# Attention followed by a mixture of experts, one core: other buffers and another order at the hand-over, and one more weight split on GpSimd

## The chip, the cores and the metric

The kernel runs on one core of one Trainium2 chip. The metric is the device time of one execution in microseconds, as the median of several runs; the profile is of one further execution of the same program. The engines are named as in the profile: PE is TensorE (PEld its weight loads), DVE is VectorE, ACT is ScalarE, POOL is GpSimd, and SP issues most of the DMAs.

## What is computed

Eight batches of eight heads, 576 positions, head dimension 64: rotary embedding, softmax attention, and then, on the 4608 rows of 512 columns that come out, a mixture of eight experts in which each row goes to the one expert with the largest gate logit. Input scales (`q`, `k`, and the output gate) are raised by constant factors, so that rounding in a single pass would change which expert is chosen.

```python
q_rot, k_rot = (rotate(q), rotate(k))
scores = scale * np.matmul(q_rot, k_rot.transpose(0, 1, 3, 2))
scores = scores - np.max(scores, axis=-1, keepdims=True)
attn = np.exp(scores)
attn = attn / (np.sum(attn, axis=-1, keepdims=True) + 1e-09)
out = np.matmul(attn, v)                      # (8, 8, 576, 64) -> x (4608, 512)
...
logits = x @ w_gate
e_idx = np.argmax(logits, axis=1)
gate_w = probs[np.arange(N), e_idx]           # softmax of logits
eom = 1.0 / (1.0 + np.exp(-(x @ w_output_gate)))
for e in range(E):
    mask = e_idx == e
    h = np.maximum(x[mask] @ w1[e], 0.0)
    ye = h @ w2[e]
    out[mask] = gate_w[mask, None] * eom[mask, e, None] * ye
```

## The kernel before

**Attention half.** The work is cut into 32 pairs of heads (8 batches, 4 pairs each), numbered from 0, and each pair into 9 row units. A unit's scores `sc` (L502) are sums of products of high and low parts (`kh`, `kl` against `q`, which holds both parts of the queries); DVE takes the row maximum `m` (L507), ACT the exponential `pm` (L516), DVE a blockwise transpose `pt` (L522), and PE the product with the values into `acc`: 288 small matmuls a pair (L544, forms of 160 and 128 columns). Behind a pair ACT evicts `acc` to `ac`, PE turns it back to rows with the matrix `ii` (the step `back`, L559), and DVE divides it into `xb` (`divide`, L571), the rows of the layer's input `x` together with the gate numbers.

Ahead of a pair, SP loads its raw queries and keys as two DMAs of 0.59 MB each into one tile `raw` of two buffers (`load`, L433: t = 1 the key half, t = 0 the query half). GpSimd multiplies and adds the rotary factors in place (L445 and behind it), and ACT and GpSimd write the high and low parts (L419, L427): `kl` is the last reader of the key half, `q` the last reader of the query half. SP also loads `v` (`loadv`, L440, four DMAs a pair).

What is issued when is a table: `EVENTS` gives for each step of a pair an offset in row units from the pair's start, and `att.step(g)` issues everything that stands at unit g. `att.G` is the unit behind the last pair's last maximum; `att.rest(...)` issues what is left over after it. The steps that the change names stand there as

```python
("load1", -18, 1), ("load0", -15, 1), ... ("loadv0", 5, 2), ("loadv1", 7, 2),
("evict", 17, 2), ("newxb", 18, 1), ("back", 19, 1), ("divide", 19, 2),
```

`place` finds for the rows of a batch the places in the expert lists and issues the stores of `xb` to `xd` in DRAM (L667, L669), three a batch, from which GpSimd gathers the experts' rows later. Of the last batch the list steps stand in `att.last`: first the one-hot rows `ro` (ACT, L719 and L720, five pairs of instructions), then the products with them, and `lists` (L746) at the end.

**MoE half.** The lists are worked off in 26 slots, a double one of 256 rows or a single one of 128. The first 5 doubles are made from the lists of the first six batches and so may begin before the last batch is through; behind them come 9 doubles mixed with 12 singles. A slot gathers its rows `xg` by GpSimd (L1039), PE transposes them (`turn`, `mtp` L1069), ACT and DVE copy them as high and low `xt` (L1084, L1085), four first products `ph` follow (`first`, L1096 and L1104), a relu on ACT, and four second products `py` (`second`, L1146), which GpSimd scatters to `out` (L1158). In a single slot the relu rows are transposed by PE in between (`across`, tile `htp`, L1131) and copied by ACT and DVE as `ht` (L1132, L1133). Each of a slot's eight weights `wr` is loaded by SP (L1052), eight loads ahead, and split six ahead into `wh` (ACT, L1061) and `wl` (L1063); `wl` is DVE's work, and in single slots GpSimd takes two of the eight (j = 1 and 5).

**PSUM.** The scores have a pool of two tiles of their own, `ps_s`; `acc` stands in `ps_a`. A small ring `Small` gives its tiles to `mtp`, `htp` and the list steps alike. When the scores are through, `ps_s` is closed, and the small ring and `ph` move to its place.

**The hand-over.** It is written out by hand: `moe.begin0` (the expert numbers `0ei`, four weights, the gathers of slots 0 and 1), the first transposes `turned_in(0, 0)`, the leftovers of attention up to unit G+1 with `back` of pair 30, `turned_in(0, 1)`, `turn`, three splits, the product of pair 31, `first(0, 0)`, `back` of pair 31 and the list product, then `first(0, 1)` and the slots.

## Time and profile before

| what | value |
|---|---|
| median of 3 runs | 1017.67 us (1014.06 to 1022.49) |
| profiled execution | 1021.62 us, of which the span is 1019.8 |
| mean granted clock of PE | 0.992 |
| busy: PE, PEld, DVE, ACT, POOL | 94%, 83%, 79%, 64%, 59% of the span |
| HBM | 198.64 MB read, 22.43 MB written, 217 GB/s |
| the hand-over | about 490 to 530 us in the span |

The span is the time from the first to the last instruction in the trace; the rest of an execution's time, 1.8 us here, lies around it. PE's 94% is an average over two halves and holds matmuls that wait for a part of their operands; it doesn't say in which places PE is late. Clock figures such as 0.82 are shares of PE's full speed.

### The profile page before, as it was taken

How to read it: one execution, taken by the hardware profiler on the slowest of the kernel's cores; microseconds unless marked ns; L12 is line 12 of the kernel's file. 1: busy time of each engine (PE TensorE's matmuls, PEld its weight loads, DVE VectorE, ACT ScalarE, POOL GpSimd, SP SyncE). 2: the span in 40 equal slices, each digit the busy share in tenths (PEclk: the TensorE clock that was granted, in tenths of full speed). 3: DMA queues.
4: the chain of work that ended last, by engine and by line, in shares of the span. 5: the costliest groups of instructions: out<-in, count | busy, mean ns of one | idle time of the engine just before them, and what ended most of it. 6: DMA issues, size and time to landing. Idle time of an engine off the chain costs nothing.

```text
span 1019.8 us, 34668 instructions
## 1 busy us (share of the span) xinstructions
PE 960.9 (94%) x14461; PEld 842.6 (83%) x14461; DVE 801.0 (79%) x1186; ACT 657.2 (64%) x1370; POOL 604.2 (59%) x626
## 2 busy tenths in 40 slices
PE   4989999989999999898889999999999999999995
PEld 4778878878878788787788898898998989898894
DVE  6779988989989899898759777667777776867772
ACT  4656677777867768676465455457567765856762
POOL 4768998998999989989521113135315343533621
PEclk9989999999999999999999999999999999999998
DMA  6546566566746757654559767768787887988860
GB/s 223 159 124 189 170 186 175 164 194 173 219 129 206 214 150 202 186 178 120 182 198 340 280 201 240 217 193 300 289 305 234 330 291 251 343 277 267 301 238 30
DMA packets 58208, 221.00 MB, mean 217 GB/s; under 512 B 9351, under 2 KB 9660, under 8 KB 53952
## 3 DMA queue, kind: packets, MB, share of 16 engines
q1 hardware_dynamic: 50304, 196.37, 61.2%
q0 software_dynamic: 6464, 21.26, 5.5%
q8 instruction: 115, 1.88, 0.8%
q10 hardware_dynamic: 1280, 1.11, 0.3%
q14 instruction: 45, 0.37, 0.1%
HBM read 198.64 MB, written 22.43 MB: 217 GB/s over the span
## 4 chain that ended last, share of the span: by engine, by line
PE 42%; DVE 3%; issue 3%; DMA 2%; ACT 1%; POOL 1%; POOLq 0%; ACTq 0%; DVEq 0%
PE py L1146 18%; PE ph L1104 15%; PE ph L1096 5%; DVE wl L1063 2%; PE mtp L1069 2%; DMA wr<-in_w 1%; PE acc L544 1%; PE htp L1131 1%; DMA out<-y,2idx 1%; PE sc L502 1%; ACT wh L1061 1%; DVE ht L1133 0%; PE acc L559 0%; DVE ht L1121 0%; DVE xt L1085 0%
## 5 line engine op out<-in xcount | busy, mean ns | idle before, releaser
L516 ACT ACTIVATE pm<-sc,m 128x576 f32<-128x576 f32 x288 | 211.8, 739 | 138.0 <-DVE m L507 119.3
L1063 DVE TENSOR_TENSOR wl<-wr,wh 128x1024 fp32r<-128x1024 f32 x184 | 253.9, 1392 | 44.5 <-ACT wh L1061 42.5
L507 DVE TENSOR_REDUCE m<-sc 128x1 f32<-128x576 f32 x288 | 206.7, 753 | 50.0 <-PE sc L502 48.2
L502 PE MATMUL sc<-kh,q 64*128 64x288 f32 x1024 | 202.5, 327 | 22.4 <-ACT q L419 9.4
L1146 PE MATMUL py<-wh,ht 128*128 128x512 f32 x640 | 214.4, 400 | 0.0
L544 PE MATMUL acc<-pt,v 32*64 32x160 f32 (+1 forms) x9216 | 201.0, 298 | 14.0 <-issue 9.0
L1061 ACT CAST wh<-wr 128x1024 fp32r<-128x1024 f32 x208 | 212.6, 1050 | 0.9 <-DMA wr<-in_w 0.9
L522 DVE STREAM_TRANSPOSE pt<-pm 128x576 f32<-128x576 f32 x288 | 207.2, 753 | 0.0
L502 PEld LDWEIGHTS sc<-kh,q 64*128 64x128 f32 x1024 | 151.1, 192 | 52.6 <-ACT pm L516 19.1
L544 PEld LDWEIGHTS acc<-pt,v 32*64 32x64 f32 x9216 | 160.0, 132 | 39.3 <-issue 30.4
L445 POOL TENSOR_TENSOR raw<-raw,rt 128x1152 f32<-128x1152 f32 x62 | 164.1, 2647 | 0.2
L1104 PE MATMUL ph<-xt,wh 128*128 128x256 f32 x896 | 160.8, 282 | 0.5 <-DVE xt L1085 0.5
L1104 PEld LDWEIGHTS ph<-xt,wh 128*128 128x128 f32 x896 | 138.2, 188 | 2.6 <-DVE xt L1085 1.4
L1146 PEld LDWEIGHTS py<-wh,ht 128*128 128x128 f32 x640 | 120.3, 188 | 24.1
L502 PE MATMUL sc<-kl,q 64*128 64x288 f32 x512 | 128.8, 305 | 0.5 <-issue 0.5
L1104 PE MATMUL ph<-xt,wl 128*128 128x256 f32 x448 | 125.8, 281 | 0.0
L1146 PE MATMUL py<-wl,ht 128*128 128x512 f32 x320 | 125.0, 391 | 0.0
L1063 POOL TENSOR_TENSOR wl<-wr,wh 128x1024 fp32r<-128x1024 f32 x24 | 58.7, 2444 | 86.7 <-ACT wh L1061 83.0
L1120 ACT ACTIVATE ht<-ph 128x512 fp32r<-128x512 f32 x56 | 33.5, 598 | 86.3 <-PE ph L1104 86.3
L449 POOL TENSOR_TENSOR raw<-raw 128x576 f32<-128x576 f32 x62 | 87.8, 1416 | 1.8
L502 PEld LDWEIGHTS sc<-kl,q 64*128 64x128 f32 x512 | 87.4, 193 | 0.2 <-DVE kl L427 0.2
L1104 PEld LDWEIGHTS ph<-xt,wl 128*128 128x128 f32 x448 | 84.4, 188 | 0.1
(249 smaller groups left out, 1323.7 us busy)
## 6 DMA issues: line engine op xcount, KB each, us to landing
wr<-in_w SPq DMA_DIRECT2D x208, 512.0 KB
raw<-in_qk SPq DMA_DIRECT2D x64, 576.0 KB
v<-in_v SPq DMA_DIRECT2D x128, 288.0 KB
xd<-xb SPq DMA_DIRECT2D x16, 640.0 KB
xd<-xb SPq DMA_DIRECT2D x8, 160.0 KB
rt<-in_rope ACTq DMA_DIRECT2D x1, 576.0 KB
xg<-xd,2idx POOLq DMA_INDIRECT x18
out<-y,2idx POOLq DMA_INDIRECT x18
```

The lines of the kernel that those rows point to most:

```text
L445: self.eng(eng).tensor_tensor(out=rv, in0=rv, in1=self.rt[:, 2 * t:2 * t + 2, x], op=ALU.mult)
L449: self.eng(eng).tensor_tensor(out=r[:, 2 * t, x], in0=r[:, 2 * t, x], in1=r[:, 2 * t + 1, x], op=ALU.add)
L502: self.nc.tensor.matmul(self.ps[i][:, a, :HS], st, mov[r, x], start=(n == 0), stop=(n == 2))
L507: nc.vector.tensor_reduce(self.m[i], ps[:, :, :HS], axis=AX.XY, op=ALU.max, negate=True)
L516: nc.scalar.activation(pe.rearrange("p (a b) -> p a b", a=2), self.ps[i][:, :, :HS], AF.Exp, bias=self.m[i], scale=1.0, accum_out=self.z[: ...
L522: self.nc.vector.transpose(out=self.pt[:, st[0] + 5 * st[1] if st else 4, :], in_=self.pc.pop(i))
L544: nc.tensor.matmul(self.acc[h * D:h * D + D, a, o:o + 32 * n], self.v[r, h, j, :], self.pt[r, u:u + n, 32 * j:32 * j + 32], start=(j == 0) ...
L1061: self.nc.scalar.copy(wh, r)
L1063: eng.tensor_tensor(out=wl, in0=r, in1=wh.bitcast(F32), op=ALU.subtract)
L1096: nc.tensor.matmul(ph[:, 0, :], st[:, dc, 0:P], mv[:, dc, :], start=(n == 0), stop=(n == 11))
L1104: nc.tensor.matmul(ph[:, f, :], st[:, dc, fs], mv[:, dc, :], start=(n == 0), stop=(n == 11))
L1146: self.nc.tensor.matmul(py[h], st[:, f, hs], mv, start=(f == 0 and n == 0), stop=(f == 7 and n == 2))
```

## The change

There are seven edits.

1. The tile `raw` is replaced by two, `raw1` (keys) and `raw0` (queries), of two buffers each, from a new pool `pr2` that stays open to the end. Each half is a tile that its load waits for by itself.
2. The first four weights of every eight (`u % 8 < 4`) are loaded into these `raw` buffers. The first four of all are issued from the attention's table, at the places where a pair 32 and a pair 33 would load their halves; `begin0` no longer stands at the hand-over.
3. The `acc` of the last pair gets a pool of its own, `ps_e`, in the scores' banks; the small ring and `ph` move to the place of `ps_a`, which is closed behind `back` of pair 30. With it the order of the hand-over changes: leftovers up to unit G+4 stand ahead of the transposes of slot 0.
4. The gathers of slot 1 stand behind `lists` and behind a copy of one element, `past`, that reads the last pair's `ac`.
5. The `xd` stores of batches 6 and 7 are issued in the slots (pieces 30, 34, ... of the list of leftovers), and no longer ahead of them.
6. The tile `htp` has two banks of its own in the pool `pm`, and no longer comes from the small ring.
7. In a single slot GpSimd also makes the `wl` that is split at j = 3. (The split is six ahead: this is the second weight of the next slot, so that it is an addition where that is a double one, which happens seven times.)

```diff
@@ the pools
-    early, main, scores = ExitStack(), ExitStack(), ExitStack()
+    early, main, scores, sums, ends = (ExitStack() for _ in range(5))
...
+    pr2 = pool(ctx, "pr2", 2, side="right")
     pp1, pp2 = pool(early, "pp", 1, side="right"), pool(early, "pp2", 2, side="right")
-    ps_a = pool(main, "ps_a", 1, space=PSUM, side="left")
+    ps_a = pool(sums, "ps_a", 1, space=PSUM, side="left")
@@ the hand-over
         att.at(g + 6, 2, moe.fetch)
+        for u, k in enumerate(("load1", "load0", "load1", "load0")):
+            att.at(att.G + 9 * (u // 2) + dict((n, o) for n, o, _ in EVENTS)[k], 1, lambda u=u: moe.load(u))
+    moe.raws = pr2
...
-        moe.begin0()
     for g in range(att.G, att.G + TURN):
         att.step(g)
     scores.close()
-    small.move(pool(ctx, "ps_x", 2, space=PSUM, side="right", reuse_waits="tile"))
-    moe.ph = pool(ctx, "ps_h", 1, space=PSUM, side="right", reuse_waits="tile")
+    att.pairs[-1].ps_a = pool(ends, "ps_e", 1, space=PSUM, side="right", reuse_waits="tile")
+    att.rest(lambda g: g <= att.G + 1)
+    sums.close()
+    small.move(pool(ctx, "ps_x", 2, space=PSUM, side="left", reuse_waits="tile"))
+    moe.ph = pool(ctx, "ps_h", 1, space=PSUM, side="left", reuse_waits="tile")
...
+        att.rest(lambda g: g <= att.G + 4)
         moe.turned_in(0, 0)
-        att.rest(lambda g: g <= att.G + 1)
         moe.turned_in(0, 1)
...
         att.rest(lambda g: True)
+        nc.gpsimd.tensor_copy(moe.t([1, 1], "past"), att.pairs[-1].ac[0:1, 0, 0, 0:1])
+        moe.gather(1)
         main.close()
         moe.first(0, 1)
+    ends.close()
     moe.open_left(pool(ctx, "ml", 1, side="left", reuse_waits="tile"),
-                  pool(ctx, "ps_m", 1, space=PSUM, side="left", reuse_waits="tile"))
+                  pool(ctx, "ps_m", 1, space=PSUM, side="right", reuse_waits="tile"))
     if n0:
         left = att.last + pieces(moe.table1(), 72)
+        for k, f in enumerate(att.later):
+            k = 30 + 4 * k
+            left[k] = lambda f=f, g=left[k]: (g(), f())
@@ the raw halves
+    @staticmethod
+    def rawtile(pr2, t, name):
+        return pr2.tile([P, 2, S], F32, tag=f"raw{t}", name=name)
...
     def load(self, t):
-        if t:
-            self.raw = self.pp2.tile([P, 4, S], F32, tag="raw", name=f"raw{self.nm}")
-        self.nc.sync.dma_start(out=self.raw[:, 2 * t:2 * t + 2, :], in_=self.qkd[:, 2 * t:2 * t + 2, :])
+        self.raw[t] = self.rawtile(self.pr2, t, f"raw{self.nm}_{t}")
+        self.nc.sync.dma_start(out=self.raw[t], in_=self.qkd[:, 2 * t:2 * t + 2, :])
@@ the stores of the last two batches
-    stores = lambda: [store(i) for i in range(3)]
     if last:
+        later += [lambda i=i: store(i) for i in range(3)]
...
-        fs += [(37, 2, lambda: (s13(), stores()))]
+        fs += [(37, 2, s13)]
+        later += [lambda i=i: store(i) for i in range(3)]
@@ the weights
         self.gather(0)
-        self.gather(1)
...
-        self.wr[u] = self.buf("wr", u, self.LOADS, 4, [P, 1024], F32, f"wr{u}{self.nm}")
+        if u % self.LOADS < 4:
+            t = Pair.rawtile(self.raws, 1 - u % 2, f"wr{u}{self.nm}")
+            self.wr[u] = t.rearrange("p a b -> p (a b)")[:, 0:1024]
+        else:
+            self.wr[u] = self.buf("wr", u, self.LOADS, 4, [P, 1024], F32, f"wr{u}{self.nm}")
...
-    def split(self, u):
+    def split(self, u, help=False):
...
-        eng = self.nc.gpsimd if self.todo[s][0] == 1 and j % 4 == 1 else self.nc.vector
+        eng = self.nc.gpsimd if help or self.todo[s][0] == 1 and j % 4 == 1 else self.nc.vector
@@ the relu rows of a single slot
-        tp = self.small.tile(f"htp{s}_{j}{self.nm}")
+        tp = self.pm.tile([P, 4, P], F32, tag=f"htp{j % 2}", name=f"htp{s}_{j}{self.nm}")
@@ the slot
-            self.split(u + self.LEAD)
+            self.split(u + self.LEAD, single and j == 3)
```

How this moves instructions is shown at three places. A row reads: line, operation, what it writes and reads, and its shape. The numbers behind names tell tiles of the same name apart.

**SP in the first pairs, with the engines that each row waits for.** The `v` tiles are those of pairs 1 and 2, the `raw` rows the two halves of pair 4, which use a buffer of pair 2. Before:

```order
L440 DMA v_462<-in_v 32x2304 [waits DMAHW2_49]
L440 DMA v_462<-in_v 32x2304 [waits DMAHW3_49]
L433 DMA raw_607<-in_qk 128x1152 [waits DMAHW4_49,Pool_49]
L433 DMA raw_607<-in_qk 128x1152 [waits DMAHW5_49]
L440 DMA v_754<-in_v 32x2304 [waits DMAHW6_49,PE_49]
```

After, the same place:

```order
L456 DMA v_469<-in_v 32x2304 [waits DMAHW2_49]
L456 DMA v_469<-in_v 32x2304 [waits DMAHW3_49]
L449 DMA raw_1_614<-in_qk 128x1152 [waits DMAHW4_49,Pool_49]
L449 DMA raw_0_687<-in_qk 128x1152 [waits DMAHW5_49,Pool_49]
L456 DMA v_762<-in_v 32x2304 [waits DMAHW6_49,PE_49]
```

Before, the key half's row waits for `Pool` for the tile as a whole, and the query half follows it; now each row has a wait for `Pool` of its own.

**PE and SP at the hand-over.** First PE, before: `acc_9652` is pair 30 and `acc_9961` pair 31, `mtp_0` and `mtp_1` are the transposes of slot 0.

```order
L544 MATMUL acc_9652<-pt_9209,v_9455 64x128
L544 MATMUL acc_9652<-pt_9209,v_9455 64x160
L1069 MATMUL mtp_0_9917<-ident,xg 128x128 x4
L559 MATMUL acc_9652<-ii,ac_113 128x160 x5
L1069 MATMUL mtp_1_9935<-ident,xg 128x128 x4
L544 MATMUL acc_9961<-pt_9590,v_9760 64x160
L544 MATMUL acc_9961<-pt_9590,v_9760 64x128
```

After, at the same place (`acc_9696` and `acc_9964` are the two pairs now):

```order
L560 MATMUL acc_9696<-pt_9244,v_9503 64x128
L560 MATMUL acc_9696<-pt_9244,v_9503 64x160
L575 MATMUL acc_9696<-ii,ac_117 128x160 x5
L560 MATMUL acc_9964<-pt_9632,v_9806 64x160
L560 MATMUL acc_9964<-pt_9632,v_9806 64x128
```

And behind the 128th matmul of pair 31, some 45 rows later:

```order
L560 MATMUL acc_9964<-pt_9632,v_9806 64x128
L560 MATMUL acc_9964<-pt_9632,v_9806 64x160
L1089 MATMUL mtp_0_10035<-ident,xg 128x128 x4
L1089 MATMUL mtp_1_10040<-ident,xg 128x128 x4
L560 MATMUL acc_9964<-pt_9632,v_9806 64x160
```

The product of pair 31 follows `back` of pair 30 directly, and both transposes stand inside it, behind 128 of its 288 matmuls. Now SP, before; the `v` tile is pair 31's:

```order
L440 DMA v_9760<-in_v 32x2304 [waits DMAHW4_49,DMAHW5_49,DMAHW2_49,PE_49]
L440 DMA v_9760<-in_v 32x2304 [waits DMAHW3_49]
L440 DMA v_9760<-in_v 32x2304 x2
L1050 TENSOR_LOAD 0ei [waits Pool_49]
L1050 ISA x2
L1052 ISA
L1052 DMA wr_9901<-in_w 128x1024 [waits DMAHW6_49]
L1052 ISA
L1052 DMA wr_9903<-in_w 128x1024 [waits DMAHW7_49]
```

After, around the `v` tiles of pairs 30 and 31:

```order
L1072 DMA wr_9277<-in_w 128x1024 [waits DMAHW6_49,Pool_49]
L1072 ISA
L1072 DMA wr_9416<-in_w 128x1024 [waits DMAHW7_49,Pool_49]
L456 DMA v_9503<-in_v 32x2304 [waits DMAHW0_49,PE_49]
L456 DMA v_9503<-in_v 32x2304 [waits DMAHW1_49]
L456 DMA v_9503<-in_v 32x2304 [waits DMAHW2_49]
L456 DMA v_9503<-in_v 32x2304 [waits DMAHW3_49]
L1072 ISA
L1072 DMA wr_9655<-in_w 128x1024 [waits DMAHW4_49,Pool_49]
L1072 ISA
L1072 DMA wr_9729<-in_w 128x1024 [waits DMAHW5_49,Pool_49]
L456 DMA v_9806<-in_v 32x2304 [waits DMAHW6_49,PE_49]
```

The four weights `wr` went ahead of the `v` rows of pair 30 and pair 31, in twos, each with a wait for GpSimd.

**POOL at a single slot that a double one follows.** `xg` is a gather, `out` a scatter. Before:

```order
L1063 TENSOR_TENSOR wl_12225<-wr_12176,wh_12224 128x1024
L1039 DMA xg<-xd,2idx 128x640 x2
L1063 TENSOR_TENSOR wl_12296<-wr_12269,wh_12295 128x1024
L1158 DMA out<-y_12301,1idx 4608x512
L1039 DMA xg<-xd,1idx 128x640
L1158 DMA out<-y_12491,1idx 4608x512
L1063 TENSOR_TENSOR wl_12634<-wr_12571,wh_12633 128x1024
```

After:

```order
L1083 TENSOR_TENSOR wl_12266<-wr_12217,wh_12265 128x1024
L1055 DMA xg<-xd,2idx 128x640 x2
L1083 TENSOR_TENSOR wl_12337<-wr_12310,wh_12336 128x1024
L1178 DMA out<-y_12342,1idx 4608x512
L1083 TENSOR_TENSOR wl_12452<-wr_12403,wh_12451 128x1024
L1055 DMA xg<-xd,1idx 128x640
L1178 DMA out<-y_12532,1idx 4608x512
L1083 TENSOR_TENSOR wl_12675<-wr_12612,wh_12674 128x1024
```

One `wl` was added, between the scatter of a single slot and a gather.

## Rows read from the trace of the kernel before

**Rows 1.** PE's waits, whole span: engine, releaser: us in total, times, longest us.

```profile
PE acc L544 <- issue: 9.0, 11, 3.6
...
PE mtp L1069 <- DVE ht L1133: 2.8, 4, 0.8
```

**Rows 2.** Maxima of pairs 2, 3 and 31: stretch, us, DVE busy, PEclk, DMA share, GB/s.

```profile
45.81:64.67 18.86, 6.44 (x9) 0.82 0.63 184
66.72:79.40 12.68, 6.44 (x9) 1.00 0.54 147
492.45:509.92 17.47, 6.45 (x9) 0.90 0.70 237
```

**Rows 3.** PE timeline in pair 2: start, us, instructions, [idle before <- releaser].

```profile
59.08 2.39 PE L544 MATMUL acc<-pt,v 32*64 32x160 f32 x50 [3.56 <-issue]
```

**Rows 4.** DMA queues from 44.4 to 56.4 us: packets, MB, share of 16 engines.

```profile
q1 hardware_dynamic: 478, 2.36, 76.8%
```

**Rows 5.** POOL timeline of the first pairs: last readers of the two raw halves.

```profile
37.04 1.41 POOL L427 TENSOR_TENSOR kl<-raw,kh 128x576 fp32r<-128x576 f32 x1 [2.41 <-ACT kh L419]
...
42.75 1.41 POOL L427 TENSOR_TENSOR q<-raw,q 128x576 fp32r<-128x576 f32 x1 [4.29 <-ACT q L419]
```

**Rows 6.** SP timeline, 473 to 516 us: the issues at the hand-over.

```profile
473.49 18.00 SPq L440 DMA_DIRECT2D v<-in_v  x8
492.56 2.00 SPq L1052 DMA_DIRECT2D wr<-in_w  x4
515.45 0.90 SPq L667 DMA_DIRECT2D xd<-xb  x2
```

**Rows 7.** PE timeline at the hand-over.

```profile
511.98 1.63 PE L559 MATMUL acc<-ii,ac 128*128 128x160 f32 x10 [0.36 <-ACT ac L553]
...
514.74 3.74 PE L544 MATMUL acc<-pt,v 32*64 32x160 f32 x196 [0.70 <-DVE xb L571]
520.21 1.88 PE L544 MATMUL acc<-pt,v 32*64 32x160 f32 x92 [1.72 <-issue]
...
524.95 1.52 PE L559 MATMUL acc<-ii,ac 128*128 128x160 f32 x10
...
527.26 0.51 PE L1104 MATMUL ph<-xt,wh 128*128 128x256 f32 x2
...
538.86 0.60 PE L1069 MATMUL mtp<-ident,xg 128*128 128x128 f32 x4
```

**Rows 8.** ACT timeline: at the hand-over, and in a lone single slot.

```profile
514.56 2.94 ACT L1061 CAST wh<-wr 128x1024 fp32r<-128x1024 f32 x3
517.40 0.53 ACT L719 ACTIVATE ro<-row,hr 128x288 fp32r<-128x288 bf16 x1
...
747.36 1.06 ACT L1061 CAST wh<-wr 128x1024 fp32r<-128x1024 f32 x1
```

**Rows 9.** POOL timeline: pair 31's `q`, `lists`, and one weight split.

```profile
490.18 1.40 POOL L427 TENSOR_TENSOR q<-raw,q 128x576 fp32r<-128x576 f32 x1
...
528.88 0.80 POOL L746 TENSOR_TENSOR lists<-lc,lists 128x288 f32<-128x288 f32 x1 [13.46 <-ACT lc L743]
...
699.38 2.44 POOL L1063 TENSOR_TENSOR wl<-wr,wh 128x1024 fp32r<-128x1024 f32 x1
```

**Rows 10.** DVE timeline around two single slots that a double one follows.

```profile
700.47 2.43 DVE L1063 TENSOR_TENSOR wl<-wr,wh 128x1024 fp32r<-128x1024 f32 x1 [0.53 <-ACT wh L1061]
...
716.79 0.68 DVE L1085 TENSOR_TENSOR xt<-mtp,xt 128x512 fp32r<-128x512 f32 x1
...
749.94 1.23 DVE L1063 TENSOR_TENSOR wl<-wr,wh 128x1024 fp32r<-128x1024 f32 x1
...
752.89 0.69 DVE L1085 TENSOR_TENSOR xt<-mtp,xt 128x512 fp32r<-128x512 f32 x1
```

**Rows 11.** PE timeline: the first two matmuls of the two double slots.

```profile
717.60 0.40 PE L1104 MATMUL ph<-xt,wh 128*128 128x256 f32 x2
...
753.46 0.55 PE L1104 MATMUL ph<-xt,wh 128*128 128x256 f32 x2
```

More of the change, by code (lines that the diff above doesn't have):

```diff
@@ L273, in __init__ @@
         self.todo = {}
[L274 removed]
+        self.last, self.later = [], []
         at = self.at
@@ L578, in number, with place @@
     return float(b * S - m + (b * S >= m))
-def place(tc, pools, pairs, b, NT, cc, trib, oneb, cnt, xbs, xd, row, lists):
+def place(tc, pools, pairs, b, NT, cc, trib, oneb, cnt, xbs, xd, row, lists, later):
     nc = tc.nc
```

37 lines of the change are left out of this document (18 added, 19 removed).

## The prediction

> **What bounds the kernel now.** I read the list of TensorE's waits first, then stretches that hold the same work at several places, then the order of time there. TensorE waits for very little that another engine owes it: in the MoE half the largest entry is 2.8 us, four waits of the token transposes `mtp` for DVE; in the attention half, past the wait for the first query, the largest is 9.0 us in eleven waits marked "issue", where TensorE waited for nothing that the profile shows [rows 1]. So what counts is not a share of busy time but single places where TensorE is late.
>
> The second view takes the nine row maxima of one head pair: 12.68 us in an ordinary pair, 18.86 us in pair 2 and 17.47 us in pair 31, the last one [rows 2]. The maxima themselves cost the same 6.44 us each time; the other engines were waiting. In pair 2 TensorE stands still for 3.56 us with "issue" [rows 3]. In the 12 us before, the DMA engines moved 2.36 MB of `raw` and `v` in 478 packets on q1, and no packet of the instruction queue q8 [rows 4]. I read this as TensorE out of instructions, its next block queued behind data that was issued earlier. The same reading fits pair 31, where `v` is issued up to 491.5 and the four weights from 492.56 [rows 6], and the wait of 1.72 us at 520.21, right after the `xd` stores and a weight were issued from 515.45 on [rows 6, 7].
>
> The third place is a single slot followed by a double one. There DVE, not TensorE, arrives last: the lone single slot's second `xt` ends at 753.58 (752.89 + 0.69), and the double slot's first two matmuls, from 753.46 on, take 0.55 instead of the usual 0.40 us [rows 10, 11].
>
> **The change part by part.** All terms are differences against the profiled execution.
>
> *Raw buffers split in two.* Today one load pair of `raw` waits for GpSimd's `q` of the pair two before. With a tile for each half the key half waits for `kl` only. At start-up `kl` ends at 38.45 and `q` at 44.16 [rows 5], and both halves are loaded after the later one. So 0.59 MB leaves the burst in front of TensorE's instructions some 5.7 us early. The burst of 2.36 MB took about 11 us [rows 4]; a quarter less in front makes it about 2 to 3 us shorter, and the stall of 3.56 us ends about that much earlier or vanishes with the slow matmuls around it. Bounds: 0, and 18.86 - 12.68 = 6.2 us [rows 2]. I take **-4.0**, nearer the upper end, since the stall is one piece and what removes most of it removes the slow restart too. In the other pairs the same shift is some 2 us. What is left of the 9.0 us there is 9.0 - 3.6 - 1.7 = 3.7 us [rows 1, 3, 7]; bounds 0 and 3.7, taken **-1.5**, since not every one of those waits is on the path.
>
> *First four weights in raw buffers.* They replace the burst at 492.56 [rows 6]. Two go out before `v` of pair 30, where nothing else moves, at no cost: `0ei` and `v` are needed only some 15 us later. But the fourth needs the buffer of `q` of pair 31, which GpSimd finishes at 490.18 + 1.40 = 491.6 [rows 9], and `v` of pair 31 is queued on SP behind it. So `v` ends its issue near 493.7 instead of 491.5: less data in front of the instructions, but 2 us later. The two nearly cancel. Bounds: 1 us lost, if the later `v` decides; 17.47 - 12.68 = 4.8 us gained, if the pair runs like an ordinary one [rows 2]. I take **-0.5**. The two gathers taken from GpSimd's queue here free 2.6 us of an engine that then only waits.
>
> *Last product in the scores' banks.* Today pair 31's `acc` waits for DVE's division of pair 30 and starts at 514.74; TensorE's `back` of pair 30 starts at 511.98 and takes 1.63 [rows 7]. With banks of its own `acc` starts when `back` is through, at 513.6. Of its 288 matmuls, at 3.74 / 196 = 0.019 us each [rows 7], 128 end at 516.05, then come the eight transposes that used to stand around `back`, about 0.9 us, then 160 more, to 520.1. The weights' burst at this point is gone, so I put the 1.72 us wait at 0. What is late next is ACT. It now does three of the five `ro` pairs before the `xt` copies, whose transposes come only at 516.7: two `xt` of about 0.6, three `wh` of 2.94 together, two `ro` pairs of about 0.9 (0.53 and its shorter half), then, as my estimate, 1.2 for the eviction of pair 31 with its small copies [rows 8]: 516.7 + 1.2 + 2.9 + 1.8 + 1.2 = 523.8. TensorE has done `first(0,0)` by 520.1 + 2.9 = 523.0 and waits 0.8 us for it. `back` and the list product follow in 2.3 us (524.95 to 527.26 [rows 7]), so `first(0,1)` starts at 526.1 instead of 527.26. Bounds: 0 and 1.72 + (514.74 - 513.6) = 2.9 us; taken **-1.2**.
>
> *Second gathers and stores later.* The gathers of slot 1 now stand behind `past`, which waits for the eviction, and behind `lists`, done at 529.68 [rows 9]. Slot 1's first transposes come at 538.86 [rows 7], so 9 us cover them; the fifth to seventh weight also wait for `past`, some 3 us later against TensorE than now, with ACT's first use of them about as late. I cost both at nothing; if the cover fails, TensorE waits 2 to 3 us. The six `xd` stores move from before the slots to slots 2 and 3, where SP runs ahead of TensorE and the gathers that read them come in slot 3's seventh step: nothing.
>
> *Own banks for `htp`.* This takes away the 2.8 us [rows 1]. But at those four places DVE is behind, and the double slot needs DVE's second `xt`, which ended at 717.47 with TensorE there at 717.60 [rows 10, 11]; a TensorE 0.7 us earlier would wait there. Alone: 0 to -2.8, taken -0.5.
>
> *One more GpSimd split.* In seven single slots followed by a double one a `wl` of 1.2 us moves from DVE to GpSimd, where it takes 2.4. The two exclude each other: GpSimd's ran from 699.38 to 701.82, and a DVE `wl` begun at 700.47 took 2.43 us, 1.08 past the other's end [rows 9, 10]. In a lone single slot ACT has this weight ready at 748.42 (747.36 + 1.06 [rows 8]), so GpSimd holds DVE's next `wl` (749.94, ready then [rows 10]) until about 750.85: it ends at 751.95 instead of 751.17, and everything behind it, up to the second `xt` at 753.58, is 0.8 us later. TensorE is waiting for just that: 3 x 0.8 = 2.4. Behind two singles DVE is late anyway and loses one `wl` less; there I get 0.2 to 0.3 a slot after the transposes' gain is used up, 4 x 0.3 = 1.2 with the -0.5 above counted: together **+3.1** for both edits. Bounds: -2.8 (no block on the path) and 7 x 1.2 = 8.4 (each block costs a whole `wl`).
>
> Sum: -4.0 - 1.5 - 0.5 - 1.2 + 3.1 = **-4.1 us**. The profiled execution took 1021.62 (1019.8 span and 1.8 around it), 3.95 over the median of 1017.67. So 1017.5 for one like it, and 1013.5 as a median.
>
> **The rivals.** *A, the fetch waits are the bulk.* All of pair 2's excess, the 3.7 us of other waits and most of pair 31's go: -6.2 - 3.0 - 3.8 - 1.2 + 3.1 = -11.1, **1006.6**. For it: the stalls stand in data bursts each time. Against: `v` of pair 31 is issued later than now.
>
> *B, the port decides, on the other side.* The earlier `raw` half changes nothing, since the block of instructions is not queued behind data, and the seven slot ends stay: -0.5 - 1.2 + 3.1 = +1.4, **1019**. It decides from the point where GpSimd's `wl` begins later than 0.5 us after ACT's cast; each 1 us more costs 7 us, so up to 1026. The rows for the lock are plain; that the fetch is behind data is my reading. The Trainium skill, page "DMA: Bandwidth & Descriptors", section "Queues, rings and completion order", says that a DMA engine takes turns between queue rows, a packet at a time. By that rule a block of instructions waits for a few packets, the split of `raw` gives nothing, and this rival's 1019 follows; 12 us without a q8 packet speak against it here, but do not show that a request was pending.
>
> *C, the cover of slot 1 fails.* The later gathers, in a stretch where the weights fill the DMA engines, hold TensorE 2.5 us: **1016**.
>
> *D, the change does not do what it says on the path:* DVE has slack enough in the lone slots and all waits for `mtp` vanish: 3.1 turns into -2.8, **1007.6**.
>
> **How the numbers follow.** Forecast 1013.5 with chance 0.47, own range 1009 to 1018; A 0.16, B 0.22, C 0.08, D 0.07. The three runs of before spread over 8 us. Range: 1004.5 to 1021.5, which leaves out half of A, with B's upper part. About 1% (10 us) is what a measurement of this kernel tells from no change. Faster by more than that (under 1007.5): most of A, a third of D and a sliver of the forecast, 0.16. Slower (over 1027.8): B's far end, 0.03. Within: 0.81.
>
> **What would show it.** In the profile after: pair 2's nine maxima near 13 to 15 us and no 3.56 us "issue"; pair 31 still near 17; `acc` of pair 31 starting 1.6 us after `back` of pair 30 begins, with no "issue" in it; `first(0,1)` 16.1 us after the last maximum (17.3 now); no wait of `mtp` for `ht`, but a new wait of `ph` for DVE's `xt`, 0.2 to 0.9 us at seven slot starts. I am wrong if pair 2 keeps its stall (then B), if pair 31 shrinks to 13 (then A), or if `mtp` of slot 1 waits for its gather (C).

## The result and the profile after

The changed kernel took 1024.89 us (median of 11 runs, 1021.04 to 1030.05), the kernel before 1017.67 (median of 11, 1014.06 to 1023.77): ratio 1.0055, interval 1.0034 to 1.0075. A repetition gave 1.0051 (1.0020 to 1.0082). So it is slower by about 5.5 us, where 4.1 us less were forecast, and the time lies outside the range (its upper end was 1021.5).

The profiled execution of the changed kernel took 1021.04, its fastest of 11 and 3.9 us under its median; that of before took 1021.62, 4 us over its median. The two profiles side by side thus show no difference where the medians differ by 7. That is why several executions of each layout are set beside each other below. (Two profiled executions, one of the kernel before and one of the version with own weight buffers, ran at a clock of 0.76 and 0.57 throughout and are left out.)

First TensorE's waits in the changed kernel, whole span; they answer to [rows 1].

```profile
PE ph L1124 <- DVE xt L1105: 6.8, 8, 1.5
PE acc L560 <- issue: 6.8, 8, 2.6
...
PE sc L518 <- issue: 2.9, 3, 1.6
```

The waits of `mtp` for `ht` are gone. In their place eight waits of `ph` for `xt` stand first, 6.8 us: seven at the starts of double slots and one, of 1.5 us, at the start of slot 1. "issue" fell from 9.0 to 6.8 us here.

The nine maxima of pairs 2, 3 and 31 (stretch, its length, DVE busy, clock, DMA share, GB/s), as in [rows 2]:

```profile
45.54:58.97 13.43, 6.44 (x9) 1.00 0.62 170
61.59:74.26 12.67, 6.44 (x9) 1.00 0.66 167
487.43:505.26 17.83, 6.45 (x9) 0.81 0.62 165
```

Pair 2 is down from 18.86 to 13.43 us and keeps its clock; pair 31 stayed at 17.8. Both as forecast. TensorE's timeline at the places of [rows 3], [rows 7] and [rows 11]:

```profile
60.05 0.53 PE L560 MATMUL acc<-pt,v 32*64 32x128 f32 x14 [0.94 <-issue]
...
499.09 2.96 PE L560 MATMUL acc<-pt,v 32*64 32x128 f32 x77 [2.56 <-issue]
...
507.31 1.62 PE L575 MATMUL acc<-ii,ac 128*128 128x160 f32 x10 [1.54 <-ACT ac L569]
508.87 2.45 PE L560 MATMUL acc<-pt,v 32*64 32x160 f32 x128
511.25 1.09 PE L1089 MATMUL mtp<-ident,xg 128*128 128x128 f32 x8
...
521.13 0.51 PE L1124 MATMUL ph<-xt,wh 128*128 128x256 f32 x2
...
543.83 0.38 PE L1124 MATMUL ph<-xt,wh 128*128 128x256 f32 x1 [1.51 <-DVE xt L1105]
...
750.04 0.39 PE L1124 MATMUL ph<-xt,wh 128*128 128x256 f32 x1 [0.67 <-DVE xt L1105]
```

The hand-over runs as it was worked out: pair 31's product starts 1.56 us after `back` begins (508.87 against 507.31), the eight transposes follow the 128th matmul, and `first(0,1)` begins 15.87 us after the last maximum (521.13 - 505.26; 17.34 before, 16.1 forecast). What was not forecast stands at 543.83: slot 1 waits.

SP and ACT tell why. SP's issues and ACT's casts that waited for a weight:

```profile
483.57 3.37 SPq L1072 DMA_DIRECT2D wr<-in_w  x2
487.04 2.00 SPq L456 DMA_DIRECT2D v<-in_v  x4
...
523.70 3.32 SPq L1072 DMA_DIRECT2D wr<-in_w  x5
```

```profile
527.23 1.05 ACT L1081 CAST wh<-wr 128x1024 fp32r<-128x1024 f32 x1 [0.33 <-DMA wr<-in_w]
...
531.12 1.05 ACT L1081 CAST wh<-wr 128x1024 fp32r<-128x1024 f32 x1 [1.55 <-DMA wr<-in_w]
...
533.69 1.05 ACT L1081 CAST wh<-wr 128x1024 fp32r<-128x1024 f32 x1 [1.03 <-DMA wr<-in_w]
```

The sixth weight is issued at 523.70, 2.6 us after `first(0,1)` began. In the kernel before it was issued 0.7 us ahead of it (527.26 [rows 7]):

```profile
526.60 1.49 SPq L1052 DMA_DIRECT2D wr<-in_w  x3
```

In the changed kernel ACT waits for weights six times, 3.8 us in all, and what it owes slot 1 comes late.

The third place is a lone single slot and the double one behind it. POOL and DVE (the double slot's first matmuls are the row at 750.04 above):

```profile
744.10 2.39 POOL L1083 TENSOR_TENSOR wl<-wr,wh 128x1024 fp32r<-128x1024 f32 x1 [1.28 <-ACT wh L1081]
```

```profile
745.56 2.01 DVE L1083 TENSOR_TENSOR wl<-wr,wh 128x1024 fp32r<-128x1024 f32 x1 [0.53 <-ACT wh L1081]
...
749.30 0.68 DVE L1105 TENSOR_TENSOR xt<-mtp,xt 128x512 fp32r<-128x512 f32 x1
```

GpSimd's added split ends at 746.49; DVE's, begun at 745.56, takes 2.01 instead of 1.23 us [rows 10] and ends 1.08 after it. That is the exclusion that the forecast took from [rows 9, 10], to the hundredth. DVE's second `xt` ends at 749.98, and TensorE waits for it.

### The profile page after: what moved, and what is told of

It is laid out like the page before. It is cut to its first block, busy times and chain, and to the rows that moved or that the text cites. A ratio compares the mean times of both kernels' runs of the same rounds, so it can differ in the third digit from the quotient of the medians.

```text
span 1019.3 us, 34697 instructions
## 1 busy us (share of the span) xinstructions
PE 961.6 (94%) x14461; PEld 841.5 (83%) x14461; DVE 797.6 (78%) x1179; ACT 656.4 (64%) x1370; POOL 627.8 (62%) x634
## 4 chain that ended last, share of the span: by engine, by line
PE 37%; issue 6%; DVE 4%; ACT 2%; DMA 1%; POOL 1%; POOLq 0%; SPq 0%; DVEq 0%; ACTq 0%
PE py L1166 15%; PE ph L1124 14%; PE ph L1116 4%; DVE wl L1083 2%; ACT wh L1081 2%; DVE xt L1105 1%; PE mtp L1089 1%; DMA wr<-in_w 1%; PE htp L1151 1%; DMA out<-y,2idx 1%; PE sc L518 0%; POOL pl L745 0%; PE acc L560 0%; DVE ht L1153 0%; POOLq L956 0%
## 5 line engine op out<-in xcount | busy, mean ns | idle before, releaser
L1083 DVE TENSOR_TENSOR wl<-wr,wh 128x1024 fp32r<-128x1024 f32 x177 | 249.4, 1421 | 49.4 <-ACT wh L1081 47.4
L523 DVE TENSOR_REDUCE m<-sc 128x1 f32<-128x576 f32 x288 | 206.8, 753 | 50.8 <-PE sc L518 48.5
L1124 PEld LDWEIGHTS ph<-xt,wh 128*128 128x128 f32 x896 | 138.2, 188 | 10.4 <-DVE xt L1105 9.3
L1083 POOL TENSOR_TENSOR wl<-wr,wh 128x1024 fp32r<-128x1024 f32 x31 | 75.1, 2423 | 107.1 <-ACT wh L1081 100.9
```

What stands on the lines that cost most here:

```text
L523: nc.vector.tensor_reduce(self.m[i], ps[:, :, :HS], axis=AX.XY, op=ALU.max, negate=True)
L1083: eng.tensor_tensor(out=wl, in0=r, in1=wh.bitcast(F32), op=ALU.subtract)
L1124: nc.tensor.matmul(ph[:, f, :], st[:, dc, fs], mv[:, dc, :], start=(n == 0), stop=(n == 11))
```

## The experiments

Ratios are to the kernel before, timed on the same chip in the same job, with 95% intervals. All runs stand together here; what they were for follows.

| run | ratio | interval |
|---|---|---|
| e1 before again | 1.0012 | 0.9987 to 1.0037 |
| e2 after again | 1.0051 | 1.0020 to 1.0082 |
| e3 after, no added split | 1.0026 | 1.0005 to 1.0048 |
| e4 before, two raw tiles | 0.9968 | 0.9940 to 0.9996 |
| e5 after, no copy `past` | 0.9988 | 0.9961 to 1.0015 |
| e6 after, neither | 0.9960 | 0.9930 to 0.9990 |
| e7, e14 own weight buffers, neither | 0.9951, 0.9961 | 0.9928 to 0.9973, 0.9936 to 0.9986 |
| e8 before, added split | 1.0051 | 1.0026 to 1.0075 |
| e13 after, fill of a 4-byte tile for the copy | 1.0050 | 1.0026 to 1.0075 |
| e19 after, fill of a 256-byte tile for the copy | 1.0012 | 0.9983 to 1.0041 |
| e15 as e7, one GpSimd split a single slot | 0.9932 | 0.9905 to 0.9959 |
| e16 as e7, none | 0.9958 | 0.9928 to 0.9988 |
| e17 before, one a single slot | 0.9979 | 0.9946 to 1.0012 |

And the profiled executions, cut at six points (us; worked out from each trace: the starts of the first maximum of pairs 3 and 30, the first `ph` of slot 1 and slot 2, the first of the first single slot and of the last one):

```
                          to     pair 3  pair 30 to  slot  slots   first single
                          pair 3 to 30   slot 1      1     2 to 6  to last
before                    66.7   407.7   73.6        26.46 116.49  305.37
e9  before                64.9   408.9   73.2        26.36 116.56  304.93
e10 before                65.4   410.1   70.4        26.39 116.45  304.43
e8  added split           62.2   409.4   72.9        26.36 116.45  308.81
e17 one split             61.9   409.8   73.3        26.45 116.49  302.27
e4  raw tiles             61.1   410.9   73.3        26.36 116.45  304.97
e11 raw tiles             61.3   408.7   70.7        26.52 116.56  304.78
after                     61.6   409.5   71.0        27.47 117.02  308.99
e2  after                 60.6   413.1   76.5        29.50 117.02  309.49
e3  no added split        61.0   416.6   69.2        27.97 117.02  305.40
e13 tile of 4 bytes       61.1   412.1   71.8        26.24 117.02  309.41
e19 tile of 256 bytes     60.2   408.8   72.0        26.40 116.49  308.21
e5  no copy               60.3   413.2   73.8        26.42 116.45  308.54
e6  neither               61.9   413.7   74.0        26.34 116.45  304.38
e7  own weights           61.7   412.6   72.6        26.41 116.45  304.65
e14 own weights           61.1   410.3   72.0        26.35 116.49  303.95
e15 one split             61.4   411.2   72.3        26.39 116.45  301.90
e16 no split              62.2   407.3   73.0        26.41 116.45  301.86
```

Behind the start of the last single slot 23.3 to 23.5 us are left, 23.7 to 23.8 with the added split.

The right half repeats to some tenths of a microsecond wherever the code is the same (slot 1 of the changed kernel is an exception that is taken up below); the left half varies by several from one execution to the next. So a term of the MoE half can be read from one pair of profiles, one of the attention half only from several.

### Is the stall of pair 2 the kernel's, or one execution's? (e1, e2, e9, e10)

Both kernels unchanged. Expected of the first repetitions:

> The kernel before, once more, for a second profiled execution. Theory 1: the stall of 3.56 us in pair 2 belongs to the one execution that was profiled (1021.62, 4 us over its median), and an ordinary execution has less of it; then the nine maxima of pair 2 take 13 to 16 us here, pair 3 begins 3 to 5 us earlier than 66.72, and the attention half ends near 505 instead of 509.9. Theory 2: the stall is of the kernel's making; then pair 2 takes 18 to 19 us again. Time: 1.000 by both (1014 to 1020).

> The changed kernel, once more. Its profiled execution (1021.04) was its fastest of 11, 3.9 us under the median. Theory 1: an ordinary execution of it loses 4 us more somewhere in the attention half, where waits marked issue come and go, and the MoE half from the first double slot on is the same within 1 us (453.5 us from 542.04 to 995.51). Theory 2: the MoE half differs by 3 us or more between executions. Time: ratio 1.0055, as before, 1.003 to 1.008.

and of two further executions of the kernel before, one each:

> The kernel before, one more profiled execution, for pair 2 alone (the profile of the first repetition had a clock of 0.758 throughout and tells nothing of it). Theory 1 (the stall of 3.56 us comes in some executions): pair 3 begins near 62, as in the run of the kernel before with the added split, where it began at 62.2, and no wait over 1 us marked issue stands between 45 and 62 us. Theory 2 (it is the rule): pair 3 begins near 66.7.

> As the run before it, a further execution: near 62 by theory 1, near 66.7 by theory 2; either is possible by theory 1 if the stall comes in some executions.

TensorE's timeline of e9 in pair 2:

```profile
56.95 2.39 PE L544 MATMUL acc<-pt,v 32*64 32x160 f32 x50 [1.81 <-issue]
```

The same wait is 2.33 us in e10, and 1.38 and 0.99 in e8 and e17, whose attention half is that of before. It comes in all five, ahead of the same matmul (the 607th of each trace); its size varies from 0.99 to 3.56, and the profile that the forecast used held the largest. Neither theory was right as put. Over these five, pair 3 begins at 64.2 in the mean, over the thirteen with two raw tiles at 61.2 (60.2 to 62.2). In those thirteen TensorE stands still ahead of the 607th matmul for 0.17 us at most; what is left there is a wait of 0.24 to 0.94 us, 128 matmuls further on, as in the row at 60.05 above.

**What ends these waits.** The packets of the instruction queue q8 are in the traces, and they say more than [rows 4] did, whose stretch ended at 56.4, where the packet began. DMA queues in the kernel before, from 50.1 to 56.4 us and from 56.4 to 59.1 us (packets, MB, share of 16 engines):

```profile
q1 hardware_dynamic: 161, 0.91, 69.8%
```

```profile
q8 instruction: 1, 0.02, 3.1%
q1 hardware_dynamic: 2, 0.00, 0.1%
```

One packet of 16 KB runs from 56.41 to 57.76, just when the data of `raw` and `v` are through, and TensorE goes on at 59.08. The packet at this place starts between 54.2 and 56.4 us in the five executions with one raw tile, between 51.2 and 53.3 in the thirteen with two (2.3 us earlier in the means), although TensorE passes the 479th matmul at the same time in all of them, 49.0 to 50.8. Beside the packet at most 0.06 MB of data begin to move. And it is the rule: of 216 waits over 0.3 us marked issue behind the start-up in these 18 traces, 214 end 1.19 to 1.73 us after a packet of q8 has ended. So these waits end with the arrival of instructions, and in pair 2 the instructions arrive when the data burst is over or nearly so. What no trace shows is when the packet was asked for.

e2 was timed as expected, and theory 1 is half of it: slot 1 begins 8.2 us later than in the first profile (550.2 against 542.0), but slot 1 itself also differs, 29.50 against 27.47 (there TensorE waits 2.01 us for `xt` instead of 1.51, and its clock is 0.94 over the slot instead of 1.00). Its worst place, TensorE and SP:

```profile
491.43 2.94 PE L560 MATMUL acc<-pt,v 32*64 32x160 f32 x70 [4.02 <-issue]
```

```profile
475.45 2.24 SPq L1072 DMA_DIRECT2D wr<-in_w  x2
477.79 1.86 SPq L456 DMA_DIRECT2D v<-in_v  x4
487.36 3.36 SPq L1072 DMA_DIRECT2D wr<-in_w  x2
```

TensorE stops in pair 30 from 487.41 on, just when the third and fourth weight are issued into the raw buffers; a 16 KB packet of q8 runs from 488.59 to 489.90, 1.5 us before TensorE goes on.

### The two raw tiles alone (e4, e11)

Edit 1 of the change in the kernel before: `raw` as two tiles of their own, the new pool closed with the others of attention.

```diff
-        self.nc.sync.dma_start(out=self.raw[:, 2 * t:2 * t + 2, :], in_=self.qkd[:, 2 * t:2 * t + 2, :])
+        self.raw[t] = self.rawtile(self.pr2, t, f"raw{self.nm}_{t}")
+        self.nc.sync.dma_start(out=self.raw[t], in_=self.qkd[:, 2 * t:2 * t + 2, :])
```

> The kernel before with the two raw tiles alone. Theory 1 (the median execution of before has little of pair 2's stall, so there is nothing to win): ratio 0.998 to 1.001, pair 2 near 13 to 15 us in the profile. Theory 2 (the forecast's reading, stall of the kernel's making): 0.993 to 0.997, 4 to 6 us. Theory 3 (earlier loads collide with the instruction fetch elsewhere): 1.002 to 1.006, with more waits marked issue in later pairs than the 9.0 us of before.

> The kernel before with the two raw tiles, a second profiled execution. Pair 3 begins between 60.5 and 62 by both theories. Where the gain is a steadier start: from pair 3 to the last maximum 445 to 450 us as before. If the split also takes stalls out of later pairs: under 444.

0.9968: 3.3 us faster (0.4 to 6.1), at the upper end of theory 2's ratios and a little less than its 4 to 6 us. Pair 3 begins 3.0 us earlier, and little of it is lost again by pair 30 here (410.9 and 408.7 against 409.2). e11 takes 441.8 us from pair 3 to the last maximum, under the 444 that it was to show if later stalls went too; but the five profiles with one tile take 440.8 to 444.6, so that this sign tells nothing. Over all thirteen profiles with the two tiles the stretch from pair 3 to 30 is 411.4 in the mean, 2.2 us longer than with one tile, but they spread from 407.3 to 416.6; the waits marked issue in it add up to 10.4 us in the mean, with one tile to 7.9. No gain in the later pairs is to be seen; that they lose something is likely and not settled.

### The added GpSimd split (e3, e8)

e3 takes it out of the changed kernel, e8 puts it into the kernel before:

```diff
-            self.split(u + self.LEAD, single and j == 3)
+            self.split(u + self.LEAD)
```

> The changed kernel without the added GpSimd split; the banks of htp stay. Theory 1 (the split holds DVE's next split, 0.5 to 0.8 us at each of seven slots, and uses up what the banks of htp give): the seven waits of ph for xt, 6.8 us with the one of slot 1, shrink to less than 2, and the time falls by 4 to 6 us against the changed kernel: ratio to the kernel before 0.999 to 1.002. Rival (the waits come from the banks of htp, which bring TensorE there earlier than DVE): the waits stay at 0.5 us or more each and the time falls by less than 2: ratio 1.003 to 1.006.

> The kernel before with the added GpSimd split alone; the htp tiles stay in the small ring. Theory 1 (GpSimd's split holds DVE's): the slots from the first single one on take 3 to 5 us longer in sum, ratio 1.002 to 1.005, waits of ph for xt of 0.4 to 1 us at seven slot starts. Rival (only with the banks of htp does the split hurt, since TensorE is later without them): under 1.5 us longer, ratio 1.000 to 1.001.

e3 is 2.7 us faster than the changed kernel (1.0026 against 1.0053, the mean of its two ratios; the intervals overlap), less than theory 1 had; its profile says 3.6 to 4.1 (305.40 against 308.99 and 309.49). TensorE's waits in e3 behind slot 1, from 570 to 1010 us:

```profile
PE ph L1124 <- DVE xt L1105: 1.8, 4, 0.6
```

Four of the seven stay, those behind two singles: they are the price of the banks of `htp`, and the split put the rest on top. In e8 the same stretch of TensorE's waits reads

```profile
PE mtp L1069 <- DVE ht L1133: 2.8, 4, 0.8
PE ph L1104 <- DVE xt L1085: 2.1, 3, 0.7
```

and the slots from the first single one on take 3.9 us more than the 304.9 of five profiles without it (1.0051 by the time). The second row is the three double slots behind a lone single one, which take 23.7 to 23.8 us instead of 22.9 to 23.1; those behind two single ones take 23.0 to 23.1 instead of 22.7 to 22.9. The rival falls: the split costs by itself.

### The copy `past` (e5, e6, e13, e18, e19)

e5 leaves the line out; e6 leaves out the split too. e13 turns it into a fill of the same tile, which reads nothing; e19 makes that tile larger. (e18, with a tile of 512 bytes, gave no result: the buffers of the MoE half no longer fit beside it.)

```diff
-        nc.gpsimd.tensor_copy(moe.t([1, 1], "past"), att.pairs[-1].ac[0:1, 0, 0, 0:1])
+        nc.gpsimd.memset(moe.t([1, 1], "past"), 0.0)        # e13; e19: [1, 64]
```

> The changed kernel without the one-element copy that the gathers of slot 1 stand behind (they are queued behind the list sum alone), so that the sixth weight no longer waits for GpSimd. Theory 1 (the sixth and later weights come late because of this copy, and ACT waits for them in slot 0): the sixth weight goes out about 3 us earlier against the second group of first products, slot 0 to slot 1 waits shrink, the first double slot behind slot 0 takes 26.5 us instead of 27.5 to 29.5, and the time falls by 1 to 3 us against the changed kernel: ratio to the kernel before 1.002 to 1.004. Rival (DVE is late there by itself, or the gathers are what is late): the 1.5 us wait of ph for xt at slot 1 stays, ratio 1.005.

> As the run before, and without the added GpSimd split. Theory 1 (both terms are independent): 1 to 3 us under the run without the split alone, ratio 0.999 to 1.002. Rival (what is left is lost to weights in front of the instruction fetch near pairs 30 and 31): ratio 1.002 to 1.004 and waits marked issue of 2 us or more between 470 and 510 us.

e5: 0.9988, some 6.5 us under the changed kernel (1.0053), more than expected. SP, ACT and TensorE in e5:

```profile
526.23 3.92 SPq L1071 DMA_DIRECT2D wr<-in_w  x6
```

```profile
530.31 4.85 ACT L1080 CAST wh<-wr 128x1024 fp32r<-128x1024 f32 x5
```

```profile
526.54 0.51 PE L1123 MATMUL ph<-xt,wh 128*128 128x256 f32 x2
...
548.10 0.39 PE L1123 MATMUL ph<-xt,wh 128*128 128x256 f32 x1 [0.52 <-DVE xt L1104]
```

The sixth weight goes out 0.3 us ahead of `first(0,1)`, ACT makes five casts in a row without a wait, slot 1 waits 0.52 as before and takes 26.42 us. The gathers are where they were, behind `lists`, so it was not they. The copy reads `ac`, whose place the sixth weight takes; with it that weight waits for GpSimd, which is at `lists` until 523.5. In the order of SP, the row of the sixth weight in the changed kernel and in e5:

```
L1072 DMA wr_10244<-in_w 128x1024 [waits PE_49,DMAHW3_49,Activation_49,Pool_49]
L1071 DMA wr_10242<-in_w 128x1024 [waits DMAHW3_49,PE_49,Activation_49]
```

But the slots from the second on are shorter too: 116.45 instead of 117.02. e6 is at 0.9960, faster than either theory had and 6.7 us under e3. Its profile has waits marked issue of up to 3.4 us between pair 30 and the last maximum, as the rival said, but not the rival's time.

> The changed kernel with the one-element copy turned into a fill of the same one-element tile, which reads nothing and which no weight waits for. Theory 1 (the wait costs): as without the copy, the slot behind slot 0 takes 26.4 us, ACT waits for no weight in slot 0, and the time is 3 to 6 us under the changed kernel, ratio 0.998 to 1.002. Theory 2 (the tile shifts what lies behind it in SBUF and the slots run slower): the sixth double slot takes 22.9 us as in the changed kernel and not 22.7, and half of the cost stays, ratio 1.002 to 1.004. Both may hold in part: then 26.4 and 22.9.

> The changed kernel with a fill of a tile of 64 elements (256 bytes) in place of the one-element copy. If what lies behind the tile is read more slowly because of an odd place: 116.45 us from the second double slot to the first single one, as without the tile, and a ratio of 0.998 to 1.003. If it is the tile's presence or the fill itself: 117.02 as with the small tile, ratio 1.002 to 1.007.

In the profiles e13 has both halves as separate things: slot 1 takes 26.24 (ACT waits for no weight, so no loss), slots 2 to 6 take 117.02 (the tile). With 256 bytes in place of 4, slots 2 to 6 take 116.49. Groups of TensorE's instructions from 570 to 700 us, in e13 and then in e19 (the second number behind the bar is the mean of one, in ns):

```profile
L1166 PE MATMUL py<-wh,ht 128*128 128x512 f32 x177 | 59.2, 400 | 0.0
L1124 PE MATMUL ph<-xt,wh 128*128 128x256 f32 x320 | 57.2, 282 | 0.0
...
L1166 PE MATMUL py<-wl,ht 128*128 128x512 f32 x89 | 34.9, 392 | 0.0
```

```profile
L1166 PE MATMUL py<-wh,ht 128*128 128x512 f32 x176 | 58.5, 398 | 0.0
L1124 PE MATMUL ph<-xt,wh 128*128 128x256 f32 x307 | 54.8, 281 | 0.0
...
L1166 PE MATMUL py<-wl,ht 128*128 128x512 f32 x88 | 34.3, 390 | 0.0
```

Matmuls overlap, so the loss is better taken from start to start. Over the five slots 2 to 6 a second product (`py`, 512 columns) follows the one before after 237.2 instead of 235.5 ns (`wh`) and 229.8 instead of 227.9 (`wl`), a first one (`ph`, 256 columns) after 118.8 instead of 118.5. That is 0.5% of the stretch, without a wait, and four fifths of it lie in the second products. So the place in SBUF of what lies behind the tile matters. The addresses in the programs tell what moves: with 4 bytes the pools behind the tile begin 32 bytes further on than without it, with 256 bytes 256 bytes further on. Of what the first and second products read only `wh` and `wl` move (to an odd multiple of 32 bytes with the small tile; in e5 and e19 they stand at multiples of 256); `xt` and `ht` stay. Which multiple it takes, the runs do not tell.

In the profiles the tile costs 0.5 us up to the first single slot and 0.9 behind it (309.3 in after, e2, e13; 308.4 in e5, e19). The times divide the cost of the copy otherwise. e13, rid of the wait, is no faster than the changed kernel (1.0050 against 1.0053, where theory 1 had 0.998 to 1.002 and theory 2 1.002 to 1.004), and e19, rid of both, is at 1.0012. Without wait and tile the times gain 6.5 us (e5), 4.1 (e19) and 6.7 (e6 against e3), the profiles 3.3. Each of these differences is uncertain by about 4 us, so they do not contradict the profiles; but the division into wait and tile rests on the profiles alone.

### The weights in the raw buffers, and the best version (e7, e14)

e7 is e6 with the four weights of eight in buffers of their own, issued at the hand-over, and both gathers early:

```diff
-        if u % self.LOADS < 4:
-            t = Pair.rawtile(self.raws, 1 - u % 2, f"wr{u}{self.nm}")
-            self.wr[u] = t.rearrange("p a b -> p (a b)")[:, 0:1024]
-        else:
-            self.wr[u] = self.buf("wr", u, self.LOADS, 4, [P, 1024], F32, f"wr{u}{self.nm}")
+        self.wr[u] = self.buf("wr", u, self.LOADS, 4, [P, 1024], F32, f"wr{u}{self.nm}")
```

> The raw tiles split, the last product in the scores' banks, the later stores and the banks of htp, but the first four weights of eight in buffers of their own and issued at the hand-over as before, both gathers early, no copy, no added GpSimd split. Theory 1 (the weights in the raw buffers collide with the instruction fetch in pairs 30 and 31 and cost 2 to 4 us at the median): ratio 0.993 to 0.997, 1 to 2 us under the two raw tiles alone. Rival (the weights' place makes no difference): the same as the run before this one within 1.5 us.

> The version with own weight buffers again. Ratio 0.993 to 0.998; in the profile 36.6 us from the end of the last maximum to the first double slot behind slot 0, and 421 us from the second of these to the last single slot.

0.9951 and 0.9961, against 0.9960 with the raw buffers: the weights' place makes no difference that these runs can tell. From pair 30 to slot 1 it is 72.6 us in the seven profiles with raw buffers (69.2 to 76.5), 72.5 in the four with own ones, and 72.5 in the seven with the order of before. Nothing is gained there by either edit; with the raw buffers it varies more. In e14 the 36.6 us from the last maximum to slot 1 was 39.4 instead (in e15 and e16 40.9 and 41.2): a wait marked issue, which the executions with raw buffers have ahead of the last maximum, came behind it. The later stores (edit 5) were not run alone; e7 holds them and shows no loss from pair 30 on.

### How many splits on GpSimd (e15, e16, e17)

```diff
-        eng = self.nc.gpsimd if help or self.todo[s][0] == 1 and j % 4 == 1 else self.nc.vector
+        eng = self.nc.gpsimd if help or self.todo[s][0] == 1 and j == 5 else self.nc.vector
```

e15 does this in e7, e17 in the kernel before; e16 has none on GpSimd.

> The version with own weight buffers, where GpSimd makes one split per single slot (that at j = 5) and DVE the other seven. If the exclusion of the two engines is what costs (a GpSimd split of 2.4 us keeps DVE from the 1.2 us split that it could make itself), the slots from the first single one on are 1 to 3 us shorter, ratio 0.991 to 0.995. If DVE's load is what costs (it gets 12 splits of 1.2 us more), single slots become longer, by up to 1 us each where a single one precedes, 3 to 10 us in sum, ratio 0.998 to 1.006.

> The version with own weight buffers, with no weight split on GpSimd in single slots. If the exclusion is all that matters, it is as fast as with one a slot or up to 1 us faster: 417 to 418.5 us from the second double slot to the last single one, ratio 0.992 to 0.995. If DVE is full by then (eight splits of 1.2 us, the xt and ht copies of a single slot are some 13 us in a slot of 12.5 to 13), TensorE waits for wl or xt at the single slots: 421 to 428 us, ratio 0.996 to 1.003.

> The kernel before, with one GpSimd split a single slot instead of two and nothing else. If each split costs by the exclusion, also where htp shares the small ring: 418 to 420 us from the second double slot to the last single one instead of 421.9, ratio 0.996 to 0.999. If only the banks of htp let it show: 421.5 to 423, ratio 0.999 to 1.002.

From the first single slot to the last it takes 301.9 us with none, 301.9 with one, 304.0 to 304.7 with two and 308.2 to 308.5 with two and the added one. DVE in the lone single slot of e15, which now makes the split itself:

```profile
745.75 1.23 DVE L1076 TENSOR_TENSOR wl<-wr,wh 128x1024 fp32r<-128x1024 f32 x1
...
748.70 0.68 DVE L1098 TENSOR_TENSOR xt<-mtp,xt 128x512 fp32r<-128x512 f32 x1
```

In e15 and e16 TensorE has no wait left in this stretch. DVE is not full with eight splits a slot; e17 shows the gain without the banks of `htp` (302.27 against 304.9). The times do not tell these versions apart: e15 is the lowest with 1014.19 us (median of 6, 1013.11 to 1015.4), 0.9932 of the kernel before and 12 us under the changed one by the ratios, but e16, whose slots take the same 301.9, is at 0.9958, and e7 and e14, whose slots take 304.0 to 304.7, are at 0.9951 and 0.9961. The gain of 2.4 us from taking splits off GpSimd is one of the profiles.

## Why the prediction was wrong

Terms in us, forecast and shown by the profiles (means of the columns above):

| term of the sum | forecast | shown |
|---|---|---|
| raw split, pair 2 | -4.0 | -3.0 |
| raw split, later pairs | -1.5 | +2.2, spread of 9: not settled |
| first four weights and last product | -0.5 - 1.2 | 0.0 |
| second gathers and the copy | 0 | +1.9 (wait) + 1.4 (tile) |
| banks of `htp` and GpSimd split | +3.1 | +3.5 |
| sum | -4.1 | +6.0 (timed: +5.4) |

(The 0.3 us that the added split costs behind the last column are not in it.)

**The step that failed** and can be shown is "I cost both at nothing", 3.3 of the 10 us between the two sums. The fact behind it was seen and right, the sixth weight some 3 us later against TensorE (2.6 us after `first(0,1)` instead of 0.7 ahead: 3.2), and the price "if the cover fails, TensorE waits 2 to 3 us" was near: slot 1 took 1.1 to 3.1 us longer, of which 1.0 to 1.5 are its wait for `xt` (1.51 to 2.03 us in after, e2 and e3, 0.52 in before). What was wrong was the cover: ACT's first use of these weights was taken to be "about as late", but ACT was through with its hand-over work and waited for six weights. Rival C had the price for another cause, the gathers; e5 and e13 leave them behind `lists` and the loss goes. The tile's part, 1.4 us, was in no case.

**The raw split.** The step for pair 2 was right: the instructions come behind the data, and with less data in front they come 2.3 us earlier in the means; e4 confirms a gain (0.9968). What failed is the -1.5 for the later pairs: the waits marked issue there did not shrink but are 10.4 us instead of 7.9 in the means. A reason that fits is that what is out of the way of one block of instructions stands in front of another; no run tests it. This is the largest difference of a term, 3.7 us, and the least settled. By the rule of the Trainium skill that rival B named (page "DMA: Bandwidth & Descriptors", section "Queues, rings and completion order") the split of `raw` would give nothing; the 3.0 us of pair 2 and e4's ratio speak against that here.

**First four weights and last product.** From the last maximum to slot 1 the profiles show 36.8 us instead of 38.1, near the forecast 1.2, but the stretch from pair 30 on gained nothing. What went behind the last maximum is the wait marked issue (2.3 us in the mean of the five with one tile, none in the seven with raw buffers), and what came ahead of it is the same kind of wait (4.0 us instead of 0.9). So the sum's two terms, -1.7 together, are 0 in the profiles. Rival A, which let these waits vanish, falls. (Its sum enters "the 3.7 us of other waits" with 3.0; with 3.7 it would be 1005.9.)

**Banks and split.** The mechanism was right in each part: 0.8 us behind a lone single slot, 0.2 behind two, -0.6 for the banks alone, and +3.9 for the split where 3.6 were put (2.4 + 1.2). Of the terms that were not put at nothing, this one came out nearest. Rival B, with this term and no gain from the fetch, ended at 1019, nearer than the forecast; but its reason, that the instructions do not wait behind data, is the one that pair 2 contradicts, and it held the -1.7 of the hand-over too. The lock is what the Trainium skill, page "SBUF — State Buffer", section "Who interferes with whom", states for VectorE and GpSimd where VectorE reads two SBUF operands; the row at 745.56 agrees (2.01 us, ending 1.08 behind GpSimd's). D falls.

**The base.** "The profiled execution took 1021.62, 3.95 over the median" was used as a shift for the whole sum. But the excess of that execution lay in part where the gain was taken: its pair 2 had the largest of five stalls, and its pair 3 began 2.5 us later than in the mean of the five. Against that execution two raw tiles gain 5.1 us up to pair 3 (61.6 against 66.7), against the mean 3.0; only the second could be taken off a median.

## What to carry to other kernels

A wait that is added on an idle engine is paid by whoever takes over the memory that the waiting instruction reads: follow the buffer, not only the queue. Two engines that exclude each other do not share work well: moving a split of 1.2 us to the one that needs 2.4 cost 0.2 to 0.8 us a slot here, and taking such work off it gave 2.4 us in the profiles. Before a stall in a profile is put into a sum, see whether it has the same size in a second execution. And where an engine waits for nothing that the list of waits names, look for the packets of the instruction queue around the end of the wait.

## What the runs showed of the hardware

TensorE's waits marked issue end with its instructions: 214 of 216 such waits over 0.3 us, in 18 traces, end 1.19 to 1.73 us after a packet of the instruction queue q8 has ended, and in pair 2 that packet starts when the data burst is through or nearly so.

A tile of 4 bytes ahead of the others moved the weights `wh` and `wl` by 32 bytes and made the matmuls of the slots take longer, from start to start 237.2 instead of 235.5 ns with 512 columns and 118.8 instead of 118.5 with 256 (five double slots: 117.02 instead of 116.45 us), and a tile of 256 bytes, which moves them by 256, took that away again.

Executions of one program spread over 13 us, and the longer ones tend to have the lower mean granted clock: of the kernel before, the fastest of 33 beside e1 to e4 took 1015.48 us at 0.995, the slowest 1028.49 at 0.984. The clock falls in single stretches, as in pair 2 of before (0.82, a mean of the levels 1.2 and 2.4 GHz [rows 2]), where TensorE stood still for 3.56 us, and not in pair 2 of after (1.00), where it stood still for 0.94.
